# A convolution with a gate: 16 groups of six rows a step in place of 13, a second ScalarE copy for some halves, and one hand-ordered list

## The chip, the cores and the metric

The kernel runs on one core of a Trainium2 chip. A core has five engines with instruction queues of their own: TensorE (PE in the profile, its weight loads PEld), VectorE (DVE), ScalarE (ACT), GpSimd (POOL) and SyncE (SP, which here only issues transfers). Each engine works through its queue in order and waits on semaphores for the others. The metric is the device time of one execution in microseconds, the median of the runs shown.

## The reference

The reference is a causal convolution over time with three taps two steps apart, a gate, and an output projection:

```python
B, T, D, K = (2, 16000, 256, 3)       # x: B x T x D, w: K x D x 2D, w_o: D x D, all bf16
xp = jnp.pad(x, ((0, 0), (4, 0), (0, 0)))
h = sum over i of xp[:, off_i:off_i + T, :] @ w[i]     # off = 4, 2, 0 for i = 0, 1, 2
f, g = h[..., :D], h[..., D:]
z = jnp.tanh(f) * sigmoid(g)
return z @ w_o
```

So every row of the output needs three products of 256 x 512 and one of 256 x 256.

## The kernel before

**Groups.** Time is cut into groups. A group of kind B takes 4R consecutive rows, R at most 256, as 4 interleaved series of R columns; a group of kind A takes 6R rows as 6 series. One group, P, computes the first 640 rows of the first sequence directly with the three taps. A and B use shared products: sums and differences of the input rows are formed first, each is multiplied with a weight matrix (a tap, or a sum of taps) once, and the results are combined. A block is a quarter of a group: 128 of the 512 output channels of h. A block of B takes four products ("first" F, "last" L, "zero" Z, "inf" I) for two pairs of series; a block of A takes five (F, "mid" M, L, Z, I) for three pairs. Each product is two matrix multiplications of up to 512 columns (`product`, L386).

**The steps of a block.** F is added up in a PSUM bank b. ScalarE copies it to SBUF (ss, `copy_first`, L432; letter c in the plan). In an A block M is then added to the same bank and VectorE forms the half hh = 1.5 ss - b (`halfway`, L443; h). L is added to b. VectorE forms the start of another bank, a = 3 ss + b in an A block and -2 ss + b in a B block (L454; a), and in an A block also yy = 2 hh + b in SBUF (L457; y). Z is added to b, and I to a. ScalarE then applies tanh or sigmoid to b, yy and a (`activate`, L475), which gives th and sg. VectorE multiplies them (`gate`, L494; g). TensorE multiplies the result with w_o (`out_mm`, L512; P in the plan's TensorE part). ScalarE, at the very end also VectorE, copies that to SBUF (`out_evict`, L537 and L521; e and v), and SP's queue stores it (L540).

**The input sums.** `operand` (L325) lists them. For B: m, p, d0 and d3, each of two input rows. For A: u0, u1, u2, e and f of two input rows; u3, uh and ud are u1 times a constant; then rp = f + u1, rm = e + u3 and r0 = u0 + uh are made by transfers that POOL issues and that accumulate into f, e and u0 (`BY_DMA`), and ri = u2 + ud by POOL in four quarters. VectorE makes the A sums and part of the B sums, POOL makes the others in quarters. The input arrives by transposing transfers on SP's queue (`load`, L234) into four buffers for A and four for B.

**Buffers.** m, p, u3, uh and ud have two buffers each; d0, d3, u0, u1, u2, e and f have three. In PSUM bank b has three, a two, and the output product three.

**What sets the order.** `PLAN` (L13) is a text with one line per block slot and four parts in a line: TensorE, ScalarE, VectorE, GpSimd. Each engine gets its instructions in the order of its part, line by line. The blocks themselves are mixed by rule: four B groups first, then blocks of A and of B in turn, then the last B group. A POOL sum is issued just ahead of the a sum of its line and is held behind the last VectorE instruction, or the one or two before it (a ' for each); the code gives the reason as "GpSimd reads SBUF while VectorE's sums read PSUM". Loads are issued 15 slots ahead of their need, stores as soon as their last copy is issued. There are 13 A groups, 10 B groups of 256 columns, one of 160 and one of 128.

Of the kernel before, what the change touches and what calls it, by code (L numbers as in the profile page):

```python
# [11 lines left out]

PLAN = """  # L13
 |  | m.0 d3.0 p.0 d0.0 G | 
F D D | c w |  | 
F L D | c d | a d3.1 G | wa.4 wa.3
F L Z I P P | c b e | a | wa.6
Z L F I | a b c | m.1 d0.1 p.1 a | wa.12'
F L Z I | a c b | m.2 g a | wa.5
L P F Z I | a e c b | d3.2 a | wa.2'  # L20
Z L F I | a b c | d0.2 u0.0 g a | wa.7
F L Z I | a c b | f.0 u1.0 a | wa.1
L F Z I | a c b | p.2 a u2.0 g | wa.14'
L Z F I P | a b e c | e.0 d3.3 a | wa.0
F P P Z L I | a c e e b | p.3 ud.0 g a | wa.11
L F I Z P P | a c b | u1.1 m.3 m.4 a | rp.0 ri.0'
F L Z P I P | a e e e b c | u3.0 e.1 uh.0 a d0.3 f.2 g | wa.10
F I Z L P | a c e b | u1.2 a | rm.0 ri.0'
L F Z I | a e c b | a g | r0.0
L Z I F P | a b c | u3.1 p.4 a | wa.8  # L30
Z L F P I | a b c e e | u0.1 uh.2 f.1 a d0.4 g | ri.0'
F I L P Z M P | c e a b | d3.4 u2.1 ud.1 a h | rp.1 rm.1 wa.15' wa.13' wa.9'
F Z L M I | a c e e b | g uh.1 a y h | d3.5' d3.5' ri.0'
P P Z F L I | y a b c | u3.2 e.2 a y | r0.1 ri.1 m.5
F L I Z M | a c y b | a u0.2 h | d0.5 d0.5
Z F L I M | a b c e | g a y h | r0.2 d0.5 ri.1
F P Z I L | a e c b y | g u2.2 a y | rm.2 ri.1 m.5' d0.5
F L P I Z M | a e c y b | a e.3 h | p.5
Z F I L M | a c b | g a y h | p.5 p.5 ri.1
P P F Z L I | a e e y c b | u0.3 a y | m.5 m.5'  # L40
L F I Z M | a c y b | ud.2 a u1.3 h | ri.2 ri.2'
Z P P F L I P M | a b e c e e | g u3.3 a y h | rp.2 p.5' p.6' d0.6'
F Z I L P | a e b c y | f.3 g a y | ri.2 d3.5
F L I Z M | a c y b | a u2.3 h | d3.5
Z F I L M P P | a c b e | g a y h | rp.3 rm.3 d0.6 ri.2
F Z I L P | a e e y b c | uh.3 e.4 ud.3 a y | d3.6 p.6 ri.3''
F L I Z M | a c y b | a u1.4 h | ri.3
Z F I L M P P P | a c b e | g a y h | m.6 d3.6
F Z P L I | a e y c b e e e | g u0.4 u3.4 f.4 a y | r0.3 ri.3 m.6''
F L P I Z M | a c y b | a ud.4 h | d0.6 d3.6 m.6  # L50
Z I F L | a b c | g a y | ri.3 m.6
F L P I Z M P | c a y b | u2.4 a h | ri.4' d3.6
F Z L I P M | a e e c b | e.5 uh.4 y a h | rp.4 p.6
F Z P L I | a y c b e e | g f.5 a y | rm.4 p.6' d0.6'
F P L Z M I | a c y b | g a h | r0.4 p.7 p.7 ri.4 d3.7 d3.7 m.7
F Z L P M I | a c e b e | u1.5 a y h | ri.4
I Z P L F P P | a e e b c y | u0.5 a y | ri.4
F L Z I M | a c b y | ud.5 u1.6 u2.5 a h u3.5 g | rp.5 ri.5''
F P Z L I P M | a c e e b | a y h | rm.5 d0.7 p.7
F Z I L P | a e y b c e | g uh.5 a y | m.7' ri.5  # L60
F L I Z P M | a c y b | g ud.6 a h | r0.5 ri.5' m.7'
F P Z L M I | a c b e e | e.6 uh.6 y a h | d3.7 d0.7
F P Z L I P | y e a b c | f.6 a y | m.7' ri.5
F L Z M I P | a c y b e | u0.6 g h u3.6 a | rp.6 p.7' d0.7' d0.7
F L P M Z I | a c e e e b | y a h | rm.6
Z I L F P | a y b c | u2.6 u1.7 a y g | m.8' m.8'
F P P L Z M I | a c e y b e e | g u3.7 a h | r0.6 ri.6' d3.7'
F Z L P I M | a c b | e.7 ud.7 a y h | p.8' ri.6' ri.6
F Z I L P P | a y b c | u0.7 u2.7 a y | p.8' ri.6'
F L P M Z I | a e c y e e b | uh.7 f.7 a h g | d0.8' ri.7'  # L70
Z I F L | a b c | u1.8 a y | rm.7 rp.7 m.8'
F P P L Z M I | a c e y b e | g a e.8 h | d3.8 ri.7
F Z I L M P | a c b e | g a y ud.8 h | p.8 d3.8 ri.7
F P Z I L P | a e c y b e | u3.8 f.8 a y | r0.7 d3.8' d0.8
L F I Z M P | a e c b y | a u0.8 h | d0.8 m.8
F Z P L P M I P | a c e e e b | e.9 g a y h | p.8 ri.7
Z F L I | a b c y | u1.9 g a y | rp.8 d3.8
F L I Z M P P | a c e b y | u2.8 ud.9 a h | rm.8 d0.8 d3.9'
Z F L P M P I P | a e c e e b | uh.8 g a y h | ri.8 ri.8
Z L F I | y a b e c | u3.9 u2.9 a y | r0.8 ri.8  # L80
F I Z L M P P | a c y b | f.9 u0.9 a h | ri.9' ri.8'
F L Z I M | a e e c b | g y a h | ri.9
F Z I L | y a b c e | f.10 g a y | rp.9 d0.9
F P P L Z M I | c a b y | u0.10 a h | rm.9 d0.9'
F Z I L P P M | a e c e b | e.10 g uh.9 y a h | r0.9 d3.9
F P Z L P I | a e e y b c e | m.9 u1.10 a y | ri.9' ri.9
F L I Z M P | c a e b y | p.9 a h | d0.9' d3.9' d3.9'
Z P F L I M | a b c e e | ud.10 g a y h | d0.9
F I Z P L P | a y b c | u2.10 g a y | rp.10 ri.10 d3.10 d0.10
F L I Z M | a c e y b | a u1.11 h |   # L90
Z P F L P I | a b c e | u3.10 g y uh.10 a | rm.10 ri.10'
F L P Z I M | a e c b e y | e.11 a u2.11 h | ri.10'
F I Z L P P M | c a e b | ud.11 f.11 a y u3.11 h | r0.10 ri.10'
F I Z L | a e c y b e | g uh.11 a y | d3.10 d0.10'
L P F P Z M I | a c b y | g a h | rm.11 d0.10 d3.10
F Z L I M P | a c e b | u1.12 a y h | ri.11' ri.11'
F Z I L | a e c b y | p.10 m.10 y a | rp.11 ri.11
L P F P Z M I | a c e b y e | a u3.12 u0.11 h f.12 g | d3.10
Z F P L I P M P | a c b e | a y h | r0.11 ri.11 d0.10
I F Z L P | a e y e b e c | g e.12 ud.12 y a | rm.12  # L100
F P P M Z L P I | c e a b y e | p.11 u2.12 uh.12 a h g | d3.11' ri.12'
F I L P Z M P | a c e b | y a h | d0.11 d3.11
F Z L P I | y e a b c e e | u0.12 m.11 a y | rp.12 r0.12 ri.12''
F P Z L M I | c a b y | a h g | 
F Z L P I M P | a c b e e e | a y h | d0.11 ri.12
F Z L P I | a c b e y | g a y | d3.11 ri.12
L F I Z M P | a c y b e e | a g h | 
Z F L P I P M | b c a | y a h | 
F P Z L I | a e e y b c e | y a | d0.11
F P L Z M I | c a b y | a h g | d0.11  # L110
F P L Z I P | a e c b e | a y | d3.11
F I Z L | a c y b | g a | 
L P I F Z P | a e b c e | a g | 
Z I F L P P | a c b E | a v | 
L Z I P p | a b | a g v | 
Z I P p P | a e b | v | 
H H | a e E | g v | 
R R |  |  | 
 | e | v | 
# [4 lines left out]
def kernel(  # L124
# [7 lines left out]

    nc = tc.nc
# [15 lines left out]
    LOAD = 15  # L151
# [4 lines left out]
    LEAD, TRAIL = 4, 0  # L156
    N_A = (6, 7)
    groups, of_kind = [], {"P": [], "A": [], "B": []}

    def group(kind, b, t, R):  # L160
        of_kind[kind].append(len(groups))
        groups.append(dict(kind=kind, b=b, t0=t, R=R, J=ROWS[kind]))
        return t + ROWS[kind] * R

    for b in range(B):
        t = 0
        if b == 0:
            t = group("P", b, 0, 160)
        rows = (T - t - 6 * RG * N_A[b]) // 4
        n_a, n_b = N_A[b], rows // RG - (0 < rows % RG < P)  # L170
        for n in range(max(n_a, n_b)):
            if n < n_b:
                t = group("B", b, t, RG)
            if n < n_a:
                t = group("A", b, t, RG)
        rows = (T - t) // 4
        while rows:
            t = group("B", b, t, 160 if rows % P else P)
            rows = (T - t) // 4
    As, Bs = of_kind["A"], of_kind["B"]  # L180
    mixed = [[(g, oi) for g in gs for oi in range(4)] for gs in (As, Bs[LEAD:-1 - TRAIL])]
    seq = [(g, oi) for g in Bs[:LEAD] for oi in range(4)]
    took = [0, 0]
    while took != [len(m) for m in mixed]:
        nxt = 0 if took[0] * len(mixed[1]) < took[1] * len(mixed[0]) else 1
        seq.append(mixed[nxt][took[nxt]])
        took[nxt] += 1
    seq += [(g, oi) for g in Bs[-1 - TRAIL:] for oi in range(4)]
    slot_of = {blk: n for n, blk in enumerate(seq)}
    N = len(seq)  # L190
    assert N == 4 * (len(groups) - 1) == len(slot_of)
    begin = {g: slot_of[g, 0] for g in As + Bs}
    end = {g: slot_of[g, 3] for g in As + Bs}
# [5 lines left out]
    pre_pool = ctx.enter_context(tc.tile_pool(name="pre", bufs=2))  # L199
    dif_pool = ctx.enter_context(tc.tile_pool(name="dif", bufs=3))  # L200
    sum_pool = ctx.enter_context(tc.tile_pool(name="sum", bufs=2))
    ss_pool = ctx.enter_context(tc.tile_pool(name="ss", bufs=3))
# [314 lines left out]
    def out_evict(g, rb0, jp, on_v=False):  # L517
# [21 lines left out]
        if G["out", rb0] == J // 2:  # L539
            nc.sync.dma_start(  # L540
                out=out[G["b"], t0:t0 + J * P, :].rearrange("(p j) d -> p j d", j=J), in_=osb[:]
            )

# [179 lines left out]
```

## Time and profile before

| | |
|---|---|
| time, median of 3 runs | 263.12 us (263.03 to 263.28) |
| span of the profiled execution | 261.4 us; no other time of that execution is given |
| TensorE busy | 256.5 us, 98% |
| VectorE busy | 240.5 us, 92% |
| ScalarE busy | 243.7 us, 93% |
| GpSimd busy | 136.2 us, 52% |
| granted TensorE clock | 0.999 |
| transfers | 45.20 MB, 173 GB/s on average |

Busy time is the time in which at least one instruction of the engine runs; two instructions that overlap count once. The span goes from the first to the last instruction. In the rows of a group of instructions the mean is that of one instruction, overlap included. A row of the timeline gives start, length, engine, line and operation; "x2" behind it means that two like instructions are shown in one row, and a bracket gives the idle time ahead of it and what ended it.

### The profile page before, as it was taken

How to read it: one execution, taken by the hardware profiler on the slowest of the kernel's cores; microseconds unless marked ns; L12 is line 12 of the kernel's file. 1: busy time of each engine (PE TensorE's matmuls, PEld its weight loads, DVE VectorE, ACT ScalarE, POOL GpSimd, SP SyncE). 2: the span in 40 equal slices, each digit the busy share in tenths (PEclk: the TensorE clock that was granted, in tenths of full speed). 3: DMA queues.
4: the chain of work that ended last, by engine and by line, in shares of the span. 5: the costliest groups of instructions: out<-in, count | busy, mean ns of one | idle time of the engine just before them, and what ended most of it. 6: DMA issues, size and time to landing. Idle time of an engine off the chain costs nothing.

```text
span 261.4 us, 4534 instructions
## 1 busy us (share of the span) xinstructions
PE 256.5 (98%) x1484; PEld 144.2 (55%) x1484; DVE 240.5 (92%) x401; ACT 243.7 (93%) x492; POOL 136.2 (52%) x204
## 2 busy tenths in 40 slices
PE   8999999999999999999999999999999999999993
PEld 5654565545545555555555555555555555665682
DVE  2899999999999999999999999999999999977773
ACT  4989998999999999999999999999999999999993
POOL 1033355687765577956757685643746453431100
PEclk9999999999999999999999999999999999999999
DMA  6999979999969667969895799959825574462115
GB/s 185 215 168 212 262 177 174 227 211 179 212 152 232 139 147 143 228 147 230 197 197 135 175 214 190 239 160 201 237 41 127 149 152 116 129 160 109 76 61 210
DMA packets 81663, 45.20 MB, mean 173 GB/s; under 512 B 68936, under 2 KB 70216, under 8 KB 81640
## 3 DMA queue, kind: packets, MB, share of 16 engines
q1 hardware_dynamic: 75112, 33.74, 54.6%
q0 software_dynamic: 5616, 10.23, 23.2%
q10 hardware_dynamic: 912, 0.95, 1.1%
q8 instruction: 11, 0.18, 0.3%
q14 instruction: 12, 0.10, 0.1%
HBM read 1.25 MB, written 16.38 MB: 67 GB/s over the span
## 4 chain that ended last, share of the span: by engine, by line
PE 97%; DMA 1%; DVE 0%; issue 0%
PE b L401 57%; PE o_ps L512 21%; PE a L401 16%; PE b L421 1%; PE a L421 1%; DMA xn<-in_x_dram 1%; PE tp L308 0%; DVE osb L521 0%; PE fill L248 0%
## 5 line engine op out<-in xcount | busy, mean ns | idle before, releaser
L435 DVE SCALAR_TENSOR_TENSOR a<-ss,b 128x512 f32<-128x512 f32 (+2 forms) x100 | 67.1, 672 | 7.9 <-ACT sg L475 3.1
L537 ACT CAST osb<-o_ps 128x512 bf16<-128x512 f32 x119 | 69.8, 622 | 0.8 <-PE o_ps L512 0.7
L512 PE MATMUL o_ps<-wo_sb,zz 128*128 128x256 bf16 x496 | 70.5, 273 | 0.0
L432 ACT COPY ss<-b 128x512 f32<-128x512 f32 (+2 forms) x100 | 59.6, 597 | 4.6 <-PE b L401 3.5
L512 PEld LDWEIGHTS <-zz 128*128 128x128 bf16 x496 | 48.4, 98 | 25.2 <-DVE zz L494 0.2
L401 PEld LDWEIGHTS <-w_sb 128*128 128x128 bf16 x400 | 39.0, 98 | 36.8 <-issue 0.2
L382 POOL TENSOR_TENSOR u<-u,ud 128x256 bf16<-128x256 bf16 x52 | 39.8, 772 | 24.9 <-DVE zz L494 9.1
L382 POOL TENSOR_TENSOR d<-xt 128x256 bf16<-128x256 bf16 (+2 forms) x56 | 33.4, 606 | 32.7 <-DVE zz L494 13.0
L494 DVE TENSOR_TENSOR zz<-th,sg 128x1536 bf16<-128x1536 bf16 (+2 forms) x52 | 40.9, 788 | 0.5 <-ACT sg L475 0.2
L435 DVE SCALAR_TENSOR_TENSOR yy<-hh,b 128x512 f32<-128x512 f32 x52 | 35.4, 680 | 1.9 <-PE b L401 1.8
L435 DVE SCALAR_TENSOR_TENSOR hh<-ss,b 128x512 f32<-128x512 f32 x52 | 35.4, 681 | 1.2 <-PE o_ps L512 0.5
L475 ACT ACTIVATE sg<-b 128x512 bf16<-128x512 f32 (+2 forms) x50 | 30.5, 610 | 2.1 <-PE b L401 1.4
L475 ACT ACTIVATE th<-b 128x512 bf16<-128x512 f32 (+2 forms) x50 | 30.5, 610 | 1.9 <-PE b L401 1.6
L475 ACT ACTIVATE sg<-a 128x512 bf16<-128x512 f32 (+2 forms) x50 | 31.0, 619 | 0.0
L401 PE MATMUL b<-f,wp_sb 128*128 128x512 bf16 x104 | 30.9, 379 | 0.0
L401 PE MATMUL b<-u,w_sb 128*128 128x512 bf16 x104 | 30.9, 379 | 0.0
L401 PE MATMUL a<-u,w_sb 128*128 128x512 bf16 x104 | 30.9, 379 | 0.0
L401 PE MATMUL b<-u,wa_sb 128*128 128x512 bf16 x104 | 30.9, 379 | 0.0
L401 PE MATMUL b<-e,wm_sb 128*128 128x512 bf16 x104 | 30.9, 378 | 0.0
L475 ACT ACTIVATE th<-a 128x512 bf16<-128x512 f32 (+2 forms) x50 | 30.5, 614 | 0.3 <-PE a L401 0.2
L401 PEld LDWEIGHTS <-wp_sb 128*128 128x128 bf16 x200 | 19.5, 98 | 20.1 <-issue 0.7
L401 PEld LDWEIGHTS <-wm_sb 128*128 128x128 bf16 x200 | 19.5, 98 | 17.0 <-issue 0.4
(59 smaller groups left out, 342.7 us busy)
## 6 DMA issues: line engine op xcount, KB each, us to landing
out_dram<-osb SPq DMA_DIRECT2D x26, 384.0 KB, 2.6
out_dram<-osb SPq DMA_DIRECT2D x23, 256.0 KB, 3.0
f<-u POOLq DMA_DIRECT2D x13, 256.0 KB, 3.5
e<-u POOLq DMA_DIRECT2D x13, 256.0 KB, 4.4
u<-uh POOLq DMA_DIRECT2D x13, 256.0 KB, 5.3
w_sb<-in_w_dram ACTq DMA_DIRECT2D x3, 256.0 KB, 4.1
xt<-in_x_dram SPq DMA_TRANSPOSE x25, 7.2
xn<-in_x_dram SPq DMA_DIRECT2D x1, 160.0 KB, 3.2
```

Of the source, the lines that this page charges most:

```text
L382: ins = eng.tensor_tensor(out=o, in0=a, in1=b, op=op)
L401: nc.tensor.matmul(G[bank, oi][:, :2 * R], lhsT=wmat[:, ct, osl], rhs=G[mv][:, :, ct, :R], start=which == "first" and ct == 0, stop=ct == ...
L421: nc.tensor.matmul(G[bank, oi][:, :4 * r].rearrange("p (j r) -> p j r", j=4), lhsT=w_taps[tap][:, ct, osl], rhs=xt[:, j0:j0 + 4, ct, c0 + ...
L432: nc.scalar.copy(out=G["ss", oi][:, :n], in_=G["b", oi][:, :n])
L435: return note(nc.vector.scalar_tensor_tensor(out=out, in0=in0, scalar=scalar, in1=in1, op0=ALU.mult, op1=op))
L475: nc.scalar.activation(out=G[name, dt][:, j:j + 2, :R], in_=G[bank, oi][:, :2 * R].rearrange("p (q r) -> p q r", q=2), func=(ACT.Tanh, ACT ...
L494: note(nc.vector.tensor_tensor(out=G["z"][:, dt, :, :n], in0=G["th", dt][:, :, :n], in1=G["sg", dt][:, :, :n], op=ALU.mult))
L512: nc.tensor.matmul(o_ps[:, q, :], lhsT=z, rhs=wo_sb[:, dt, :], start=dt == 0 and (q == 0 or len(dts) == NT), stop=dt == NT - 1, skip_group ...
L537: copy(out=osb[:, 2 * jp:2 * jp + 2, :], in_=o_ps[:])
```

## The change

Five things change.

- The groups are written out. There are 16 A groups, 5 B groups of 256 columns, one of 160 and two of 128. P stays.
- The order of the blocks is written out too (`ORDER`): three B groups, then four A blocks to about one B block, then a B group of 128 columns.
- `PLAN` is one list of instructions of all engines in one order; each engine still takes its own in that order. Halves, evictions, stores (s) and loads (x) name what they handle, so that they need not come in the order of the blocks. A POOL sum carries a number q: it is held behind the VectorE instruction that many places back in the list (0 is the last).
- In 17 of the 64 A blocks the half is not formed on VectorE. ScalarE copies b a second time instead, after M (token k): hh = b. There yy = -2 hh + a, where a is the bank just formed as 3 ss + b; so yy comes after a, and it reads the bank a in PSUM before I is added to it. In the other 47 blocks h stays as it was.
- The buffers of the input sums, halves, activations and output rows are given out by the number of the group (`slot`), with the same counts as before; hh has three, as it had.

```diff
+GROUPS = (
+    "P160 A A A A A A A A B B B",
+    "A A A A A A A A B B B128 B160 B128",
+)
+ORDER = """
+9 9 9 9 10 10 10 10 11 11 11 11 1 20 1 1 1 2 20 2 2 2 3 20 3 3 3 4 20 4 4 4 5 21 5 5 5 6 21 6 6 6 7 21 7 7 7 8 21 8
...
 PLAN = """
- |  | m.0 d3.0 p.0 d0.0 G | 
-F D D | c w |  | 
...
+G p.0 m.0 d0.0 F d3.0 D c D d0.1 D F d p.1 L c G F w L A c P m.1 wa.2q1 x Z A I b wa.5q3 L u1.0 a wa.7q5 Z e0 F A
...
+b I Y e47 L a A F y P A Z c g Z b M b u1.7 F k25 I u0.7 c I u3.7 a L f.8 rm.7d M a A rp.7d P k26 ud.7 F e48 Y P
...
-    def halfway(blk):
+    def second(blk, on_act):
         g, oi = blk
         G = groups[g]
         n = 2 * G["R"]
-        G["hh", oi] = ss_pool.tile([P, 2 * RG], f32, name="hh")
+        G["hh", oi] = slot("hh", a_seq.index(blk), [P, 2 * RG], f32)
+        if on_act:
+            G["k", oi] = True
+            nc.scalar.copy(out=G["hh", oi][:, :n], in_=G["b", oi][:, :n])
+            return
         stt(G["hh", oi][:, :n], G["ss", oi][:, :n], 1.5, G["b", oi][:, :n], ALU.subtract)
...
             G["y", oi] = ss_pool.tile([P, 2 * RG], f32, name="yy")
-            stt(G["y", oi][:, :n], G["hh", oi][:, :n], 2.0, b)
+            if ("k", oi) in G:
+                stt(G["y", oi][:, :n], G["hh", oi][:, :n], -2.0, G["a", oi][:, :n])
+            else:
+                stt(G["y", oi][:, :n], G["hh", oi][:, :n], 2.0, b)
...
+    SLOTS = {"m": 2, "p": 2, "d0": 3, "d3": 3, "u0": 3, "u1": 3, "u2": 3, "e": 3, "f": 3, "u3": 2, "uh": 2, "ud": 2, "hh": 3, "th": 2, "osb": 3, "odd": 3}
+    def slot(name, n, shape, dtype=bf16, kind=None):
+        return ring_pool.tile(shape, dtype, name=name, tag=f"{name}.{n % SLOTS[kind or name]}")
...
+    def on_gpsimd(token):
+        token, _, back = token.partition("q")
+        behind = made_v[-1 - int(back)]
...
+    def store(g, rb0, odd):
...
+        nc.sync.dma_start(out=to, in_=G["osb", (rb0, odd)][:])
...
+    for token in PLAN.split():
+        what = token[0]
+        if "." in token:
+            if "q" in token:
+                on_gpsimd(token)
+            elif token[-1] == "d":
+                pre(*group_of(token[:-1]), None)
+            else:
+                note(pre(*group_of(token), nc.vector))
+        elif what in "FMLZI":
+            product(next(kinds[what]), {"F": "first", "M": "mid", "L": "last", "Z": "zero", "I": "inf"}[what])
...
+        elif what in "hk":
+            second(a_seq[int(token[1:])], what == "k")
```

More of the change, by code (lines that the diff above doesn't have):

```diff
@@ L150 @@
     BRIDGE, FILL = 4, 6
-    LOAD = 15
     W_A = 4
     ROWS = {"P": 4, "B": 4, "A": 6}
-    LEAD, TRAIL = 4, 0
-    N_A = (6, 7)
     groups, of_kind = [], {"P": [], "A": [], "B": []}
[L160 to L163, printed above, removed]
     for b in range(B):
         t = 0
[L167 to L189, printed above, removed]
-    N = len(seq)
-    assert N == 4 * (len(groups) - 1) == len(slot_of)
-    begin = {g: slot_of[g, 0] for g in As + Bs}
-    end = {g: slot_of[g, 3] for g in As + Bs}
+        for word in GROUPS[b].split():
+            kind, R = word[0], int(word[1:] or RG)
+            of_kind[kind].append(len(groups))
+            groups.append(dict(kind=kind, b=b, t0=t, R=R, J=ROWS[kind]))
+            t += ROWS[kind] * R
+        assert t == T
+    seq = []
+    for word in ORDER.split():
+        g = int(word)
+        seq.append((g, sum(at[0] == g for at in seq)))
+    As, Bs = ([g for g, oi in seq if oi == 0 and g in of_kind[kind]] for kind in "AB")
+    N = len(seq)
+    assert sorted(seq) == [(g, oi) for g in range(1, len(groups)) for oi in range(4)]
+    for gs in (As, Bs):
+        for n, g in enumerate(gs):
+            groups[g]["n"] = n
+    begin = {g: seq.index((g, 0)) for g in As + Bs}
     wanted = {g: begin[g] - (6 if g in As else 0) for g in As + Bs}
@@ L276 @@
     wm_sb = consts.tile([P, CT, D2], bf16)
[L277 removed]
+    wu_sb = [[slot("hh", tap, [P, D2], f32), ss_pool.tile([P, D2], f32, name="yy")] for tap in range(K)]
     wa_sb = consts.tile([P, CT, D2], bf16)
@@ L465, in activate @@
         if (name, dt) not in G:
-            G[name, dt] = act_pool.tile([P, J, RG], bf16, name=name, tag=f"{name}{J}")
+            same = [at for at in blocks if groups[at]["J"] == J]
+            G[name, dt] = slot(f"{name}{J}", NT * same.index(g) + dt, [P, J, RG], kind="th")
         if G["kind"] == "P":
@@ L705 @@
+    assert next(todo, None) is None and next(to_load, None) is None
 _INS = ['x', 'w', 'w_o']
```

346 lines of the change are left out of this document (116 added, 230 removed).

## The prediction

> **What bounds the kernel now.** I read the page first (engines, slices, chain), then the chain in order of time, then windows of the steady part, then single instructions.
>
> ```profile
> span 261.4 us, 4534 instructions
> PE 256.5 (98%) x1484; PEld 144.2 (55%) x1484; DVE 240.5 (92%) x401; ACT 243.7 (93%) x492; POOL 136.2 (52%) x204
> ...
> PE   8999999999999999999999999999999999999993
> ...
> DVE  2899999999999999999999999999999999977773
> ACT  4989998999999999999999999999999999999993
> ...
> PE 97%; DMA 1%; DVE 0%; issue 0%
> ...
> ```
>
> The chain is TensorE from end to end. A busy TensorE alone proves little, so I check its pace in the chain in order of time:
>
> ```profile
> 11.44 0.43 PE b L401 x2
> ...
> 47.98 1.73 PE b L401 x8
> ...
> 255.12 2.20 PE o_ps L512 x20
> ...
> 257.34 0.69 DVE osb L521
> ```
>
> A 512-column product takes 1.73/8 = 0.216 us, a 256-column one 2.20/20 = 0.110 us, in proportion to the columns, so it streams without gaps. Summing the plan of the kernel before, letter by letter, with these two prices (320 columns in proportion: 0.136) gives 244.8 us for TensorE. The plan's first product starts at 11.44 and the last ends at 257.32: 245.9 us. So TensorE waits 1.1 us in the whole plan. After it come 4.1 us of last copy and store (261.4 - 257.32).
>
> VectorE is next. The windows give DVE busy in the third pair of numbers behind the length (PE, PEld, DVE, ACT, POOL):
>
> ```profile
> 20.00:60.00 40.00, 40.00 (x217) 21.00 (x215) 39.55 (x68) 37.51 (x74) 22.08 (x32) 1.00 1.10 207
> ...
> 180.00:220.00 40.00, 40.00 (x228) 22.15 (x227) 38.75 (x66) 38.56 (x78) 20.81 (x30) 1.00 0.61 143
> 220.00:240.00 20.00, 20.00 (x125) 12.01 (x123) 17.51 (x31) 19.88 (x44) 7.18 (x12) 1.00 0.46 125
> 240.00:257.40 17.40, 17.30 (x132) 12.68 (x130) 12.79 (x24) 16.89 (x42) 1.20 (x3) 1.00 0.27 105
> ```
>
> Busy time overstates the load, because one instruction's end overlaps the next one's start. What an instruction costs its engine is the distance from start to start when the next is ready:
>
> ```profile
> 9.31 0.69 DVE L382 TENSOR_TENSOR m<-xt 128x1024 bf16<-128x1024 bf16 x1
> ...
> 100.59 0.68 DVE L494 TENSOR_TENSOR zz<-th,sg 128x1024 bf16<-128x1024 bf16 x1
> 101.19 0.69 DVE L382 TENSOR_TENSOR f<-xt 128x1024 bf16<-128x1024 bf16 x1
> 101.80 0.68 DVE L435 SCALAR_TENSOR_TENSOR a<-ss,b 128x512 f32<-128x512 f32 x1
> 102.40 0.68 DVE L435 SCALAR_TENSOR_TENSOR yy<-hh,b 128x512 f32<-128x512 f32 x1
> 103.00 0.95 DVE L494 TENSOR_TENSOR zz<-th,sg 128x1536 bf16<-128x1536 bf16 x1
> 103.87 0.69 DVE L435 SCALAR_TENSOR_TENSOR a<-ss,b 128x512 f32<-128x512 f32 x1
> ...
> 113.16 0.42 DVE L380 TENSOR_SCALAR u<-u 128x1024 bf16<-128x1024 bf16 x1
> 113.50 0.95 DVE L494 TENSOR_TENSOR zz<-th,sg 128x1536 bf16<-128x1536 bf16 x1
> ...
> 253.82 0.43 DVE L435 SCALAR_TENSOR_TENSOR a<-ss,b 128x256 f32<-128x256 f32 x1
> 254.16 0.42 DVE L494 TENSOR_TENSOR zz<-th,sg 128x512 bf16<-128x512 bf16 x1
> 254.49 1.28 DVE L521 CAST osb<-o_ps 128x512 bf16<-128x512 f32 x2
> ```
>
> So on VectorE: PSUM sum of 512 columns 0.60, of 256 columns 0.34; input sum of 1024 0.61; scaling 0.34; gate of 1536 0.87, of 1024 0.60, of 512 0.33; eviction 0.60. With these the VectorE plan sums to 228.8 us, between 9.31 and 257.94: 19.8 us are free, 7.1 of them after 220 us (2.49 + 4.61 in the last two windows), 12.7 spread before.
>
> **The change, part by part.** *TensorE.* Counted in the two programs: the products of 512 columns fall from 840 to 800 (13 x 40 + 10 x 32 against 16 x 40 + 5 x 32), those of 256 columns in B groups rise from 32 to 64; 320-column products, the direct group and the 500 output products stay. -40 x 0.216 + 32 x 0.110 = **-5.1 us**, all on the path. The new list sums to 239.7 us. With today's start, waits and tail: 11.44 + 239.7 + 1.1 + 4.1 = 256.3 us of span. That is the floor.
>
> *VectorE.* PSUM sums of 512 columns: a 92 to 84, halves 52 to 47, yy 52 to 64: -1 x 0.60 = -0.6. Of 256 columns 4 to 8: +1.4. Input sums of 1024: u 39 to 48, e and f 13 to 16 each, d 10 to 8, m and p 6 to 4 each: +9 x 0.61 = +5.5. Scalings 39 to 48: +3.1. Gates: 1536 26 to 32, +5.2; 1024 20 to 10, -6.0; 512 6 to 8, +0.7. Evictions 5 to 7: +1.2. Four short B sums become one: -1.1 (estimate, 0.37 each). Sum **+9.4 us**; summed token by token the list is 238.1 (+9.3). Today this would be hidden under TensorE's 12.7 us of cover, but TensorE gets 5.1 shorter too: the cover is gone. The two lists now run side by side: at the 32nd of 96 Z products TensorE's sum is 78.5 and VectorE's 79.8, at the 64th 160.8 and 161.2, at the 88th 222.6 and 223.1. VectorE starts 2.1 us earlier (9.31 against 11.44), and that is all its lead.
>
> *ScalarE.*
>
> ```profile
> 100.40 0.58 ACT L432 COPY ss<-b 128x512 f32<-128x512 f32 x1
> 100.88 0.60 ACT L475 ACTIVATE sg<-b 128x512 bf16<-128x512 f32 x1
> ...
> 103.27 0.69 ACT L475 ACTIVATE th<-yy 128x512 bf16<-128x512 f32 x1
> 103.81 0.64 ACT L475 ACTIVATE th<-b 128x512 bf16<-128x512 f32 x1
> ...
> 253.63 0.43 ACT L475 ACTIVATE th<-b 128x256 bf16<-128x256 f32 x1
> 253.91 0.43 ACT L475 ACTIVATE th<-a 128x256 bf16<-128x256 f32 x1
> ```
>
> 0.48 for 512 columns, 0.54 from yy, 0.28 for 256. Copies ss 92 to 84, new second copies +17, activations of a and b 184 to 168, of yy 52 to 64, evictions 119 to 117: +3 x 0.48, +12 x 0.06 for the yy, +12 x 0.28 for the 256-column ones: **+5.5 us**. The list sums to about 235, starting near 11.6: done at 247 of 256, so some 9 us of cover remain and I cost it at nothing. Without that cover it would add up to its 5.5.
>
> *The second copy (17 of 64 blocks).* It takes 0.60 off VectorE and puts 0.48 on ScalarE, and adds one wait: yy now reads the a bank, so the I product, which adds to that bank, waits for Y and not for A alone. Behind I the whole TensorE queue stands, since the order is fixed. By the sums between Y's end and I's start lie 1.0 to 3.7 us in these blocks, so no cost while VectorE is less than 1 us late; beyond that the excess, at most one sum (0.60) a block, 17 x 0.6 = 10 at the very worst, 0 at best. I take 0: it is part of how late VectorE is, below.
>
> *GpSimd, queues.* POOL's sums fall from 140 to 124, many of them shorter, its accumulating transfers rise from 39 to 48.
>
> ```profile
> 105.06 0.98 DVE L382 TENSOR_TENSOR u<-xt 128x1024 bf16<-128x1024 bf16 x1
> ...
> 105.45 1.11 POOL L382 TENSOR_TENSOR u<-u,ud 128x256 bf16<-128x256 bf16 x1
> ...
> L382 POOL TENSOR_TENSOR u<-u,ud x52: 658/667/1125, 33.1 to 236.4; 128x256 bf16<-128x256 bf16 x52
> L382 DVE TENSOR_TENSOR u<-xt x39: 673/685/1215, 21.7 to 227.8; 128x1024 bf16<-128x1024 bf16 x39
> ...
> f<-u POOLq DMA_DIRECT2D x13, 256.0 KB, 3.5
> e<-u POOLq DMA_DIRECT2D x13, 256.0 KB, 4.4
> u<-uh POOLq DMA_DIRECT2D x13, 256.0 KB, 5.3
> ...
> xt<-in_x_dram SPq DMA_TRANSPOSE x25, 7.2
> ```
>
> POOL at 52% has room. From issue to first use the new list leaves 5.2 to 17 us by TensorE's sum (the old plan 3.5 to 23), against 3.5 to 5.3 to land. Loads go from 25 to 24 transposes, SP's stores from 51 to 48, each load put by hand between stores; most stand 8 us or more ahead of the first use against 7.2 to land, one (the first 128-row B group that is mixed in) only 4 us, and there POOL waits with the transfers behind it. Cost 0 with 5 us on POOL; 2 to 6 if a late accumulation stops TensorE.
>
> The old plan put every POOL sum directly ahead of an a sum and held it behind one of the last three VectorE instructions. In the new list most holds name an instruction long past, so the start is where POOL's queue happens to be. 111 of 140 POOL sums and weight sums still stand ahead of a PSUM sum, 29 ahead of another kind. The rows above show what meeting costs: u took 0.98 where 0.69 is usual, and POOL's sum 1.11. If all 29 met: 29 x 0.29 = 8.4; if none, 0. I take 9 of them, 2.6, because in the rows of u the median stays at 685.
>
> *The sum.* Let x be the time VectorE does not run at its back-to-back pace up to the 88th block. Then span = 9.31 + 223.1 + x + 17.1 (TensorE's rest) + 4.1 = 253.6 + x, or the floor of 256.3 where x is under 2.7. Lower bound: 0.45 idle in 40 us (20 to 60, the one stretch where both plans already weigh the same), 2.4 over 214 us. Upper bound: the 12.7 us that VectorE stands idle today. The lower is nearer, as much of the 12.7 is waiting for a TensorE that was the bound: 2.4 + 2.6 for POOL = 5.0. Span 258.6. No separate time of the profiled execution is given; its span is 1.7 below the median of the runs (263.12 - 261.4), and I carry that: **260.3 us**, 1.1% faster.
>
> **The rivals.** *TensorE stays the bound* (x under 2.7): 256.3 + 1.7 = 258.0. For it, the 20-to-60 stretch, where TensorE did not wait; against it, that this lasted 40 us and would have to last 215.
>
> *VectorE becomes the bound (slower).* Place: the mixed stretch from 35 to 235 us; price: x stays at what it is today, 12.7: 266.3 + 1.7 = 268.0. It decides from x = 7.8 on, where 253.6 + x passes 261.4. For it: two lists of equal length that wait for each other in fixed order, with 2.1 us of lead; against it: TensorE was the bound while VectorE stood idle, so much of the 12.7 will not come again. The Trainium skill (Perfetto Trace Analysis, section "Identifying the Most-Contended Engine") judges VectorE and ScalarE by occupancy and does not count matmul occupancy: by it the 93% and 92% are the bound and a change that adds to both loses; the trace bears this out only in part, since TensorE streams at 0.216 a product.
>
> *VectorE and POOL exclude each other (slower).* Each of the 29 meetings makes VectorE wait out a whole POOL sum (667 ns in the row above): 2.4 + 19.3 = 21.7, 253.6 + 21.7 + 1.7 = 277.0. Against it: u has 685 as median although POOL is busy half of the time, and the u at 105.06 lost 0.29. The Trainium skill (SBUF — State Buffer, section "SBUF: two separate sides") states this rule, an exclusive lock on a shared pair of ports for operations with two SBUF inputs; the trace agrees that meetings cost, at less than half of that size.
>
> *The saving is given back*: x between 7.3 and 8.3, 262.6 to 263.6.
>
> *A late transfer*: two stops of about 3 us each at fixed products, 258.6 + 6 + 1.7 = 266.3. For it, 23% more accumulations; against it, the leads above.
>
> **How the numbers follow.** TensorE the bound 0.13; my forecast, x from 2.7 to 7.3 (258.0 to 262.6), 0.50; given back 0.10; VectorE the bound 0.16; POOL excluding VectorE 0.03; late transfer 0.08. A measurement here can tell about 0.2%, 0.5 us. Faster 0.63, same 0.10, slower 0.27. The range, 257.8 to 266.2, leaves out half of VectorE's case, the whole of POOL's and half of the late transfers, 0.15; the forecast's own range is 258.0 to 262.6.
>
> **What would show it.** TensorE's busy time near 251.4 if its sum is right. VectorE at 39.5 or more of 40 us in every window from 20 to 220. New waits of TensorE's loads on VectorE's a and yy, or none. If u, e and f last over 0.75 on average, the POOL part was too small; if the waits name DMA into f, e or u, it was the transfers; if ScalarE has no idle time and others wait for ss, the 9 us of cover were wrong.

## The result, and the profile after

The changed kernel takes 290.86 us (median of 4 executions, 289.38 to 293.16) against 263.2 us for the kernel before (263.03 to 263.28): **1.105 times as long, 95% interval 1.100 to 1.110**. The forecast was 260.3 us, faster. So 27.7 us were added where 2.8 were to be saved, and the sum missed 30.6 us. Single executions far off the others of their kernel (688 to 946 us in four, 270.7 and 274.6 us in two) are left out of every time, and the profiles of e2_own, e3_pace_own and e16_no_acc_ri, which are of such executions, are not read.

The page of the kernel after (engines, three of the slices, the granted clock, the chain):

```profile
span 291.4 us, 4595 instructions
...
PE 261.5 (90%) x1476; PEld 144.6 (50%) x1476; DVE 265.7 (91%) x419; ACT 249.1 (85%) x507; POOL 126.1 (43%) x197
...
PE   8799964999794999999989989987799989998994
...
DVE  3689971899999799999999999999999999998794
...
PEclk9979996999998899999999999999999999999999
...
PE 31%; DVE 24%; issue 10%; ACT 9%; DVEq 0%; ACTq 0%
```

TensorE was the chain for 97% before and is it for 31% now, with VectorE next. VectorE is busy 25.2 us longer than before, though its list should have grown by 9.3. The windows (length; busy time and instructions of PE, PEld, DVE, ACT, POOL; granted clock, share and GB/s of the transfers) show two different troubles:

```profile
40.00:60.00 20.00, 14.03 (x67) 7.11 (x65) 11.57 (x20) 11.04 (x22) 7.14 (x11) 0.83 0.53 104
...
140.00:180.00 40.00, 37.11 (x209) 20.26 (x208) 40.00 (x64) 36.97 (x76) 19.43 (x30) 1.00 0.98 201
180.00:220.00 40.00, 35.84 (x209) 20.13 (x208) 39.97 (x62) 36.39 (x77) 20.04 (x33) 1.00 0.88 195
```

From 40 to 60 us every engine is idle for a good part of the time. From 140 on VectorE is full and TensorE is not. The count alone does not say why: the kernel before got 64 and 66 VectorE instructions done in the last two of these windows, against 64 and 62, but VectorE had 1.2 us to spare in each and TensorE none:

```profile
140.00:180.00 40.00, 40.00 (x228) 22.05 (x227) 38.85 (x64) 38.43 (x77) 26.00 (x35) 1.00 0.85 181
```

The groups of VectorE's instructions tell more (count, busy us, mean ns of one, idle time ahead); first the kernel before:

```profile
L435 DVE SCALAR_TENSOR_TENSOR a<-ss,b 128x512 f32<-128x512 f32 x92 | 63.4, 690 | 3.9 <-PE b L401 2.6 <-ACT th L475 0.6
...
L382 DVE TENSOR_TENSOR u<-xt 128x1024 bf16<-128x1024 bf16 x39 | 27.9, 720 | 0.0
L494 DVE TENSOR_TENSOR zz<-th,sg 128x1536 bf16<-128x1536 bf16 x26 | 24.8, 954 | 0.5 <-ACT sg L475 0.2
L494 DVE TENSOR_TENSOR zz<-th,sg 128x1024 bf16<-128x1024 bf16 x20 | 13.7, 683 | 0.0
...
L380 DVE TENSOR_SCALAR uh<-u 128x1024 bf16<-128x1024 bf16 x13 | 5.5, 420 | 0.0
```

And the kernel after:

```profile
L368 DVE SCALAR_TENSOR_TENSOR a<-ss,b 128x512 f32<-128x512 f32 x84 | 57.4, 686 | 11.0 <-PE b L334 10.0 <-ACT th L416 0.6 <-PE a L334 0.3
L315 DVE TENSOR_TENSOR u<-xt 128x1024 bf16<-128x1024 bf16 x48 | 39.3, 829 | 0.0
L435 DVE TENSOR_TENSOR zz<-th,sg 128x1536 bf16<-128x1536 bf16 x32 | 36.4, 1137 | 0.0
...
L313 DVE TENSOR_SCALAR uh<-u 128x1024 bf16<-128x1024 bf16 x16 | 10.8, 673 | 0.0
L435 DVE TENSOR_TENSOR zz<-th,sg 128x1024 bf16<-128x1024 bf16 x10 | 8.9, 893 | 0.0
```

Sums with one operand in PSUM kept their time (a: 690 ns before, 686 now). Much of what works from SBUF alone became longer on average: u by 109 ns, the gate zz of 1536 by 183, that of 1024 by 210, uh by 253. These means come from few instructions: over the whole timeline 23 of VectorE's lasted more than 0.1 us beyond the usual length of their row, 22.2 us together, and all 23 overlap a GpSimd sum; the rest kept their length. In the kernel before there were 7, worth 1.8 us. The rise of uh is a single instruction, and the timeline of VectorE and of GpSimd (start, length, engine) shows what it waited for:

```profile
86.76 0.68 DVE L368 SCALAR_TENSOR_TENSOR hh<-ss,b 128x512 f32<-128x512 f32 x1
87.36 4.55 DVE L313 TENSOR_SCALAR uh<-u 128x1024 bf16<-128x1024 bf16 x1
91.83 0.68 DVE L368 SCALAR_TENSOR_TENSOR hh<-ss,b 128x512 f32<-128x512 f32 x1
...
86.43 0.96 POOL L315 TENSOR_TENSOR p<-xt 128x256 bf16<-128x256 bf16 x1
87.06 1.57 POOL L315 TENSOR_TENSOR u<-u,ud 128x256 bf16<-128x256 bf16 x2
88.31 0.94 POOL L315 TENSOR_TENSOR p<-xt 128x256 bf16<-128x256 bf16 x1
88.94 0.93 POOL L315 TENSOR_TENSOR u<-u,ud 128x256 bf16<-128x256 bf16 x1
89.56 0.93 POOL L315 TENSOR_TENSOR p<-xt 128x256 bf16<-128x256 bf16 x1
90.19 1.43 POOL L315 TENSOR_TENSOR d<-xt 128x256 bf16<-128x256 bf16 x2
```

The half hh, one operand in PSUM, runs beside GpSimd in its usual 0.68 us. The scaling uh, from SBUF to SBUF, takes 4.55 us instead of 0.42 and ends 0.3 us after GpSimd's run of sums does. GpSimd had saved up these sums while it waited, and nothing held them any more behind a late VectorE instruction.

The stop at 40 us is another thing. The waits (engine, line, waited for what; us, times, longest) and the instruction that waited:

```profile
PE b L334 <- DVE hh L368: 10.7, 6, 3.8
...
ACT hh L378 <- POOL wa_sb L231: 6.4, 1, 6.4
PE b L334 <- ACT hh L378: 6.0, 1, 6.0
```

```profile
45.74 1.07 POOL L231 TENSOR_TENSOR wa_sb<-hh 128x128 bf16<-128x128 f32 x1
...
46.84 0.59 ACT L378 COPY hh<-b 128x512 f32<-128x512 f32 x1 [6.37 <-POOL wa_sb L231]
```

The first second copy k0 writes a buffer of the ring hh. The scratch of the weights (wu_sb) lies in the same three buffers, so k0 must wait until GpSimd has formed the last piece of wa, at the end of its queue of those 40 us. TensorE stands behind k0 for 6.0 us, and its granted clock is 0.50 from 45.5 to 52.2 us: a product that took 0.59 us before the stop takes 1.06 there. The kernel before kept the scratch in the same three buffers; there the first half came at 47.85 us, beside the last sums of wa (46.94 to 48.33), and TensorE ran on.

### The profile page after: what moved, and what is told of

Read it like the earlier page. It is cut to its first block, busy times and chain, and to the rows that moved or that the text cites. A ratio compares the mean times of both kernels' runs of the same rounds, so it can differ in the third digit from the quotient of the medians.

```text
span 291.4 us, 4595 instructions
## 1 busy us (share of the span) xinstructions
PE 261.5 (90%) x1476; PEld 144.6 (50%) x1476; DVE 265.7 (91%) x419; ACT 249.1 (85%) x507; POOL 126.1 (43%) x197
## 4 chain that ended last, share of the span: by engine, by line
PE 31%; DVE 24%; issue 10%; ACT 9%; DVEq 0%; ACTq 0%
PE b L334 18%; PE o_ps L453 8%; DVE a L368 6%; PE a L334 5%; DVE yy L368 5%; DVE hh L368 4%; DVE zz L435 3%; DVE u L315 3%; ACT osb L470 2%; ACT th L416 2%; ACT sg L416 2%; ACT ss L365 2%; DVE e L315 1%; DVE u L313 1%; DVE uh L313 1%
## 5 line engine op out<-in xcount | busy, mean ns | idle before, releaser
L368 DVE SCALAR_TENSOR_TENSOR a<-ss,b 128x512 f32<-128x512 f32 (+2 forms) x96 | 62.6, 655 | 11.0 <-PE b L334 10.0
L315 POOL TENSOR_TENSOR u<-u,ud 128x256 bf16<-128x256 bf16 x64 | 49.1, 810 | 34.0 <-DVE u L315 24.5
L334 PE MATMUL b<-f,wp_sb 128*128 128x512 bf16 x128 | 38.5, 382 | 16.7 <-DVE hh L368 10.7
L435 DVE TENSOR_TENSOR zz<-th,sg 128x1536 bf16<-128x1536 bf16 (+2 forms) x50 | 48.7, 973 | 0.6 <-ACT sg L416 0.6
L334 PE MATMUL b<-u,w_sb 128*128 128x512 bf16 x128 | 38.6, 385 | 3.5 <-DVE a L368 2.8
L334 PE MATMUL a<-u,w_sb 128*128 128x512 bf16 x128 | 38.6, 383 | 2.4 <-DVE a L368 2.2
L315 DVE TENSOR_TENSOR u<-xt 128x1024 bf16<-128x1024 bf16 x48 | 39.3, 829 | 0.0
L334 PE MATMUL b<-e,wm_sb 128*128 128x512 bf16 x128 | 38.3, 381 | 0.0
L334 PE MATMUL b<-u,wa_sb 128*128 128x512 bf16 x128 | 38.2, 384 | 0.0
L310 POOL DMA_DIRECT2D e<-u x16 | 15.6, 977 | 42.3 <-PE b L334 27.0
```

The lines of the kernel that those rows point to most:

```text
L310: return nc.gpsimd.dma_start(out=G[name][:, :, :, :R], in_=b, accum_op=op)
L315: ins = eng.tensor_tensor(out=o, in0=a, in1=b, op=op)
L334: nc.tensor.matmul(G[bank, oi][:, :2 * R], lhsT=wmat[:, ct, osl], rhs=G[mv][:, :, ct, :R], start=which == "first" and ct == 0, stop=ct == ...
L368: return note(nc.vector.scalar_tensor_tensor(out=out, in0=in0, scalar=scalar, in1=in1, op0=ALU.mult, op1=op))
L435: note(nc.vector.tensor_tensor(out=G["z"][:, dt, :, :n], in0=G["th", dt][:, :, :n], in1=G["sg", dt][:, :, :n], op=ALU.mult))
```

## The experiments

All are compared with the kernel before, on the same chip (263.1 to 263.4 us in each batch). The times of most repaired kernels spread by 1 to 4 us, so a difference of 1 us between two of them tells nothing.

**The weights' scratch out of the halves' buffers (e2_own).** It shares the buffers of the six-row output rows instead.

```diff
-    wu_sb = [[slot("hh", tap, [P, D2], f32), ...
+    wu_sb = [[slot("osb6", tap, [P, D2], f32, kind="osb"), ...
```

> The changed kernel, with the scratch of the A weights taken out of the buffers of the halves (it shares the buffers of the 6-row output rows instead). Theory P (ports): two faults add up, the first second copy waits 6 us for GpSimd's weight sums (and TensorE behind it), and GpSimd's sums that start where the queue happens to be hold VectorE up for some 20 us. Here only the first goes: 283 to 286 us, and the stop of 6 us near 41 us is gone; u stays above 0.80 us and the gate of 1536 above 1.08. Theory L (lists): the two lists of equal length simply cannot both run dense; the early stop is only moved, and the time stays above 288.

Measured: 284.1 us (281.5 to 284.9), 1.076 [1.070, 1.082]. So the wait of k0 costs 6.8 us, the 6.0 of the row and a little more. Its own lengths and waits are not shown; in e4, built on it, TensorE is busy for 18.69 of the 20 us from 40 to 60, against 14.03.

**GpSimd paced again (e3_pace_own).** With e2's edit, every GpSimd sum is also held behind the VectorE instruction just ahead of it in the list; the numbers q are ignored.

```diff
-        behind = made_v[-1 - int(back)]
+        behind = made_v[-1]
```

> As the run before, and every GpSimd sum is held behind the last VectorE instruction ahead of it in the list (q = 0 for all), which is the pacing of the kernel before. Theory P: u comes down to 0.75 or less and the gate of 1536 to 1.00 or less, and the time to 264 to 271 us. Theory L: the means fall too, but the time stays above 278, since VectorE only waits elsewhere.

Measured: 270.1 us (269.9 to 271.4), 1.027 [1.024, 1.030]. One line gives back 14.0 us. The lengths are read in e4 below, which has the same hold: u falls from 829 to 734 ns, the gate of 1536 from 1137 to 1014.

**The opposite in the kernel before (e7_before_free).** All its GpSimd sums are held behind VectorE's first instruction, which means not at all.

```diff
-            behind = made_v[-1 - token.count("'")]
+            behind = made_v[0]
```

> The kernel before, with the hold of every GpSimd sum set to VectorE's first instruction, so that GpSimd starts as soon as its operands are there; nothing else is changed. Theory P: the gate of 1536 goes from 0.954 us to above 1.02 and u from 0.72 to above 0.78, VectorE loses 8 to 15 us, of which 12 are covered today: 264 to 272 us. Theory L: the means stay within 0.03 us and the time within 1 us of 263.

Measured: 315.4 us, 1.197 [1.196, 1.199]. VectorE's groups in this kernel:

```profile
L435 DVE SCALAR_TENSOR_TENSOR a<-ss,b 128x512 f32<-128x512 f32 x92 | 63.0, 687 | 9.4 <-PE b L401 8.7 <-ACT th L475 0.4
L494 DVE TENSOR_TENSOR zz<-th,sg 128x1536 bf16<-128x1536 bf16 x26 | 39.1, 1504 | 0.8 <-ACT sg L475 0.7
...
L494 DVE TENSOR_TENSOR zz<-th,sg 128x1024 bf16<-128x1024 bf16 x20 | 25.9, 1297 | 0.0
```

The direction was expected, the size by far not: the holds are worth 52 us to a kernel that changes in nothing else. The a sums stay at 687 ns; the gates go from 954 to 1504 and from 683 to 1297. 47 instructions are longer than usual by over 0.1 us, 48.8 us together against 1.8 before, and all of them overlap a GpSimd sum. This is the clearest evidence for the cause, since neither groups nor lists differ from the kernel before.

**GpSimd's sums placed just ahead of PSUM sums (e4_align_own).** On top of e3, a GpSimd sum waits in the list until the next a, yy or half, at the latest until the product that needs it.

```diff
+        elif "." not in token and what in "AYh" and waiting:
+            on_gpsimd(waiting.pop(0))
...
-                on_gpsimd(token)
+                waiting.append(token)
```

> As the run before, and each GpSimd sum also waits in the list until the next a, yy or half sum of VectorE comes, one GpSimd sum ahead of each. Theory P: below the run before by 1 to 4 us, 260 to 269, u at 0.72 or less. Theory L: like the run before, above 278.

Measured: 271.2 us (269.4 to 272.8), 1.026 [1.022, 1.030]: no gain over e3 that could be told. Being held behind any late VectorE instruction is what counts. Meetings are left, but shorter ones: 28 instructions, 8.0 us together.

**Two tries to let GpSimd meet PSUM sums alone (e8_two_own, e13_halves).** In e8 (built on e3) a sum is only put where two PSUM sums follow each other; e13 (built on e12_both, below) cuts it in two where just one does.

```diff
+            if waiting and (two or len(waiting) > 4 and "." not in token and what in "AYh"):
+                on_gpsimd(waiting.pop(0))
```

```diff
+                if part is None and big and not two and len(waiting) < 5:
+                    on_gpsimd(token_, 0)
+                    waiting[0] = (token_, 1)
```

> As the aligned kernel, but a GpSimd sum is issued only where two PSUM sums of VectorE follow each other (or where more than four are waiting), since a GpSimd sum (0.67 us) is longer than one PSUM sum (0.60). If the rest of VectorE's loss is the overhang: u at 0.71 or less, gate of 1536 at 0.98 or less, 264 to 269 us. If GpSimd then comes late for TensorE: 270 to 276.

> As the run before, and a GpSimd sum of 256 columns is cut into two of 128 (0.40 us in place of 0.67) wherever the PSUM sum that covers it is not followed by another. Theory P: what is left of VectorE's longer instructions is the overhang of the GpSimd sum into the next VectorE instruction: the gate of 1536 goes to 0.97 or less, u to 0.70 or less, 3 to 5 us off, 259 to 263 us. If GpSimd comes late instead: 266 or more.

Measured: 297.1 us, 1.128 [1.126, 1.131], and 285.7 us, 1.086 [1.082, 1.089]. Both made it worse. The waits of e8:

```profile
PE a L334 <- POOL u L315: 18.4, 16, 3.1
```

and of e13:

```profile
PE a L339 <- POOL u L320: 16.2, 16, 3.1
```

TensorE's I product now waits for ri, once in each of the 16 groups. There are not enough such places: a more careful pacing makes GpSimd late.

**VectorE's share of it (e6_no_k, e9_more_k).** Both are e4 with another number of second copies on ScalarE: none instead of 17, which puts 17 halves of 0.60 us back on VectorE, and 30 instead of 17. The edit of e6:

```diff
-            second(a_seq[int(token[1:])], what == "k")
+            second(a_seq[int(token[1:])], False)
```

> The paced and aligned kernel with all 64 halves on VectorE (no second copies). If VectorE's back-to-back work is now the bound, its 17 x 0.60 = 10 us come in full or nearly: 276 to 282 us. If waits are the bound and not VectorE's work: 268 to 273.

> The aligned kernel with 13 more second copies on ScalarE (30 of 64). If VectorE is the bound: 13 x 0.60 = 8 us less for it and 6 more for ScalarE, 263 to 267 us. If ScalarE or the waits are the bound: 269 to 275.

Measured: 279.65 us, 1.063 [1.061, 1.065] without them, 8.4 above e4 for 10.2 us of work; 272.8 us, 1.037 [1.035, 1.039] with 30, 1.6 above. So the 17 copies are worth about their price, and more of them bring nothing: in two windows of e9_more_k

```profile
60.00:100.00 40.00, 38.76 (x216) 20.92 (x215) 37.21 (x61) 38.59 (x79) 25.20 (x36) 1.00 0.74 165
100.00:140.00 40.00, 39.72 (x218) 20.95 (x216) 38.63 (x64) 39.83 (x82) 20.18 (x30) 1.00 0.84 175
```

VectorE has room (37.21 and 38.63 of 40), and ScalarE is the fuller of the two (38.59 and 39.83).

**Loads earlier, first gate later (e10_loads, e12_both).** In e4 a load for a B group came late. e10 moves the last four loads for B groups up by two or three places; e12 also puts the first gate, which VectorE reaches first and must wait for, behind three input sums.

```diff
+    for late, ahead in ((21, 5), (23, 12), (22, 15), (24, 17)):
+        loads.remove(late)
+        loads.insert(loads.index(ahead), late)
...
-G p.0 m.0 d0.0 F d3.0 D ...
+m.0 p.0 d0.0 G F d3.0 D ...
```

> The aligned kernel (269 to 272 us) with the loads of the four mixed B groups put one to three places earlier among the loads; nothing else. Theory D: the stop near 175 us, where GpSimd waits for a late load and TensorE for the transfer of r0 behind it, is a cost of its own: 265 to 268 us. Theory V: VectorE's work alone sets the time, and the stop is made up elsewhere: 269 or more.

> As the run before, and the first gate of group P comes behind the sums m, p and d0 of the first B group, as in the kernel before, where it stood first in the list and waited for ScalarE. Theory S: the 2.2 us that TensorE loses in the first 20 us come back: 2 us below the run before, 263 to 266. Theory V: no difference beyond 0.5 us.

Measured: 272.8 us, 1.036 [1.034, 1.039], and 271.3 us, 1.033 [1.028, 1.037]. Nothing was gained. A stop of TensorE between 180 and 190 us went (busy 8.48 of 10 us in e4, 9.88 in e12), and another came between 200 and 210 (9.77 in e4, 6.68 in e12). The window of e12_both there, then its timeline and the transfers issued from 185 to 206 us (KB each, median us from issue to landing):

```profile
200.00:220.00 20.00, 16.68 (x98) 9.38 (x97) 17.23 (x29) 16.81 (x37) 10.08 (x17) 1.00 0.68 146
```

```profile
187.36 10.80 SPq L169 DMA_TRANSPOSE xt<-in_x_dram  x2
...
193.51 0.88 POOL L313 DMA_DIRECT2D e<-u  x1 [0.86 <-DVE e L318]
...
203.65 0.60 PE L337 MATMUL b<-e,wm_sb 128*128 128x512 bf16 x2 [3.32 <-DMA e<-u]
```

```profile
e<-u POOLq DMA_DIRECT2D x1, 256.0 KB, 10.1
xt<-in_x_dram SPq DMA_TRANSPOSE x2, 9.6
...
e<-u POOLq DMA_DIRECT2D x16, 256.0 KB, 4.3
```

An accumulation into e was issued at 193.51, while two transposing loads were running, and landed after 10.1 us; the last row gives 4.3 us as the median over the whole execution. TensorE stood 3.3 us for it. Moving a load moved the meeting, and with it the stop.

**GpSimd's last sums away (e5_no_ri, e14_no_ri_fixed).** The 64 sums of ri are left out, in e4 and in e12, to measure the contact that is left between GpSimd and VectorE. These kernels and those below no longer compute the reference's output.

```diff
+        if name == "ri":
+            return None
```

> The paced and aligned kernel of the runs before, with GpSimd's 64 quarters of ri = u2 + ud left out (the I products of the A blocks then read u2 alone). It measures what is left of GpSimd's sums. If what remains above the floor is VectorE and TensorE waiting on GpSimd (VectorE's longer instructions, 8 us, and TensorE's waits on POOL and DMA, 5 us): 258 to 263 us, u at 0.71 or less. If the two equal lists alone cost it: 267 or more.

> The kernel of the two fixes (loads and first gate), with GpSimd's 64 quarters of ri left out (the I products of the A blocks read u2 alone). The lists with almost no GpSimd: if the two equal lists can run side by side, 259 to 262 us, the prediction's own sum (260.3); if not, 264 or more.

Measured: 269.3 us, 1.022 [1.018, 1.026], and 270.8 us, 1.025 [1.018, 1.032]: 1.9 and 0.6 us, where about 10 had been expected. The idea that the rest was still GpSimd beside VectorE alone fell with this. u is down to 687 ns, and TensorE's waits in e14_no_ri_fixed now name transfers:

```profile
PEld L339 <- DMA e<-u: 6.2, 3, 3.4
...
PE b L339 <- DMA e<-u: 4.9, 3, 2.9
```

**The accumulating transfers away, with controls (e15_no_acc, e16_no_acc_ri, e20_no_acc_ri_again, e17_before_no_acc_ri, e18_before_no_acc).** rp, rm and r0 are left as f, e and u0; e16, e17 and e20 leave out ri too. e17 and e18 are the kernel before, the others e12; e20 is the same kernel as e16.

```diff
         if eng is None:
+            return None
+        if False:
             return nc.gpsimd.dma_start(out=G[name][:, :, :, :R], in_=b, accum_op=op)
```

> The repaired new list with its first gate moved and four loads earlier (269 to 272 us) without the 48 accumulating transfers (rp, rm and r0 are left as f, e and u0, so the output is not the reference's); GpSimd's sums for ri stay. Theory T, late accumulations are what holds the repaired list up: the stop in the slice from 200 to 220 us goes (TensorE over 19 of 20 there, 16.7 with the transfers), 260 to 264 us. Theory V, VectorE and the lists' order hold it: 268 to 272, and the waits of TensorE name VectorE.

> The same without the 64 GpSimd sums for ri as well (u2 is left as it is, so the output is not the reference's): two lists without transfers and nearly without GpSimd. T: 257 to 261 us, the floor of the prediction's sum. V: 267 to 270, as without ri alone (270.8).

> The run without accumulations and without the sums for ri again (262.1 us), for a profile of it: if VectorE's list at its limit is the rest, VectorE is busy 39.5 or more of 40 us in the windows from 60 to 220 us with means of its sums as in the kernel before (u 690, gate of 1536 columns 955 ns), and TensorE is not; if TensorE is the bound, its chain is TensorE for over 90% as in the kernel before.

> The kernel before, without its 39 accumulating transfers and its GpSimd sums for ri (output not the reference's): the control for the run above. Both theories: TensorE waited for 1.1 us in the whole plan, so 262 to 263.5 us. If the new list without both lies below this one, the saving of 5.1 us on TensorE is real and the side streams hid it; if it lies above, it is VectorE's list.

> The kernel before without its 39 accumulating transfers, GpSimd's sums for ri kept (output not the reference's): 262 to 263.5 us by both theories; more than 1 us below 263.2 would say that transfers cost the kernel before too.

| without | new list, repaired (e12) | kernel before |
|---|---|---|
| nothing | 271.3 us | 263.1 us |
| accumulations | 265.6 us, 1.010 [1.008, 1.012] | 263.6 us, 1.002 [1.001, 1.003] |
| accumulations and ri | 262.1 and 262.5 us, 0.997 [0.996, 0.998] | 263.0 us, 1.000 [0.998, 1.001] |

The side streams cost the kernel before nothing, and the repaired new list 9.2 us. Taken alone, ri was worth 0.6; once the accumulations are away it is worth 3.5, so the two are not to be priced one by one. The window of e15_no_acc where e12 stopped:

```profile
200.00:220.00 20.00, 19.89 (x120) 11.42 (x118) 19.96 (x35) 19.94 (x44) 6.98 (x13) 1.00 0.17 63
```

What is left without both is a draw of two lists. The windows of e20_no_acc_ri_again:

```profile
60.00:100.00 40.00, 40.00 (x230) 22.32 (x229) 40.00 (x68) 39.74 (x81) 10.09 (x17) 1.00 0.57 145
100.00:140.00 40.00, 40.00 (x223) 21.48 (x221) 39.84 (x68) 39.65 (x81) 4.26 (x9) 1.00 0.47 122
140.00:180.00 40.00, 38.87 (x231) 22.33 (x230) 38.54 (x68) 39.02 (x83) 8.39 (x18) 1.00 0.51 124
180.00:220.00 40.00, 40.00 (x235) 22.69 (x233) 39.86 (x71) 40.00 (x87) 5.46 (x13) 1.00 0.42 123
```

TensorE, VectorE and ScalarE are all full or nearly so, with 68 to 71 VectorE instructions in 40 us. The chain is TensorE for 85%, below the 90% of the expectation, and VectorE for 6%; no engine alone is shown as the bound.

**Late landing or late issue (e19_no_late_loads).** In e12, 16 of the 24 loads are left out; the groups read rows of an earlier group again.

```diff
+        if G["kind"] != "P" and len(filled[J]) == 4:
+            G["xt"] = [xt for xt, rows in filled[J] if rows >= R][G["n"] % 2]
+            return
```

> The repaired new list with its first gate moved and four loads earlier (269 to 272 us), with 16 of its 24 transposing loads left out: those groups read the rows of an earlier group again, so the output is not the reference's. All sums and accumulations stay. Theory C, the accumulations land late because a transposing load fills the transfer engines beside them: the 48 accumulations all land in under 7 us (9 to 10 at the stops with the loads), the stop between 200 and 220 us goes, 265.5 to 268 us, near the run without accumulations (265.6). Theory R, they are late because VectorE or GpSimd issues them late: 269 to 272 us, and the stop stays.

Measured: 267.9 us (267.2 to 268.1), 1.018 [1.017, 1.020]: 3.4 of the 5.7 us. The window, and the accumulations' median landing over the execution:

```profile
200.00:220.00 20.00, 19.44 (x113) 10.76 (x112) 19.97 (x34) 19.54 (x42) 10.04 (x17) 1.00 0.46 113
```

```profile
e<-u POOLq DMA_DIRECT2D x16, 256.0 KB, 3.6
u<-uh POOLq DMA_DIRECT2D x16, 256.0 KB, 3.4
```

The stop is gone, with GpSimd's issues waiting for TensorE's products on bank b as long as in e12 (25.1 us in 9 waits in both). The accumulation into e that was issued at 193.51 us in e12 is issued at 193.55 here, after the same wait, and lands after 4.0 us in place of 10.1; its row for the time from 193.4 to 194 us:

```profile
e<-u POOLq DMA_DIRECT2D x1, 256.0 KB, 4.0
```

So this stop comes from an accumulation that lands beside transposing loads. The other 2.3 us of the accumulations have not been told apart.

No version that computes the reference's output beat the kernel before; the best were e3_pace_own, e4_align_own and e12_both at 270.1 to 271.3 us.

## Why the prediction was wrong

Going down the chain of runs, the 30.6 us between 260.3 and 290.9 are: 6.8 for k0 and the weights' scratch (e2), 14.0 for unpaced GpSimd (e3), -1.2 for placement, loads and gate (e4 and e12, which gained nothing), 5.7 for the accumulations (e15), 3.5 for ri behind them (e16), and 1.8 between the lists alone and the forecast (262.1 - 260.3). Each is the price at its place in this order.

- **The step that failed first is "GpSimd, queues".** It saw that most holds name an instruction long past, and then counted neighbours in the list (29 of 140), let 9 of them meet and priced a meeting at 0.29 us: 2.6 us, where pacing gave back 14.0. Without a hold the list says nothing of when GpSimd runs, so any VectorE sum, gate or scaling on SBUF can meet it: 11 of 48 u sums and 10 of 32 gates of 1536 did, and they lasted 1.32 us against 0.68 and 1.55 against 0.95 of those that met nothing. These are means of meetings that cost nothing and of meetings that cost up to 2.1 us, for VectorE waits out what GpSimd has lined up; the scaling uh lost 4.1 us. The 23 that became longer lost 0.96 us each, more than a whole GpSimd sum (median 667 ns in the kernel before). The step also took from the u median of 685 in the kernel before that few of them would meet. It was the pacing that kept the meetings rare there, which e7 shows: 52 us.
- **The rival "VectorE and POOL exclude each other"**, given 0.03, had the right mechanism. The Trainium skill (SBUF — State Buffer, section "SBUF: two separate sides") has the shared port pair as an exclusive lock, and names the VectorE operations that need it: those with two SBUF inputs and those in a two-port fast mode. The trace agrees, with the PSUM sums at 686 ns and the gates at 1137; whether uh, which has one input, runs in such a mode no run here shows. The rival's price, 19.3 us for 29 meetings of 667 ns, is near the 22.2 measured by luck: there were fewer long meetings, and each cost more. The argument against it, that u kept its median while GpSimd was busy half of the time, was drawn from a kernel built to avoid the meetings.
- **"The second copy", taken at 0.** The step looked at the wait of I for Y and did not ask whose buffers k writes. The new list puts the first half ahead of the last weight sums, whose scratch lies in the halves' buffers: 6.8 us, at one place. By the code a half on VectorE would write the same buffer, so it would be the place in the list that costs, and not the engine; no run tests that.
- **"Cost 0 with 5 us on POOL; 2 to 6 if a late accumulation stops TensorE."** The upper case came true in the repaired list: 5.7 us. In the changed kernel itself TensorE's longest wait for an accumulation is 0.5 us. The leads of 5 us and more that the step counted were fair against a median landing of 3.5 to 5.3 us, not against the 10.1 us of the one beside two transposing loads.
- **The list term, x = 2.4 without GpSimd, was too small as well.** The counts of instructions on the three engines are as the prediction has them. With the side streams away the sum would say the floor, 256.3 us of span; e20 has 260.5, so x in "span = 253.6 + x" is 6.9, of which 1.1 us are meetings that are left. The 1.8 us in the chain above look small only because the forecast holds 2.6 for GpSimd. The new list gains 0.5 to 0.9 us over the kernel before without its side streams (262.1 and 262.5 against 263.0), not the 5.1 of TensorE. Which waits make up the rest stays open.
- **VectorE the bound** came true from 140 us on, by waiting and not by work: VectorE's busy time is 265.7 us in the kernel after and 245.4 in e20 for the same 419 instructions. The Trainium skill (Perfetto Trace Analysis, section "Identifying the Most-Contended Engine") judges VectorE and ScalarE by their occupancy. At 92% and 93% in the kernel before they had little room for anything to be late, as the full windows of e20 show.

Of the signs that were named, u, e and f did last over 0.75 us on average (829, 793 and 743 ns, 805 over all 80), which meant that the GpSimd part was too small. TensorE's busy time, named as near 251.4 us, was 261.5, and 253.9 in e20.

## What to carry to other kernels

When a list is rewritten, ask of every wait what else it did beside keeping the order: here the holds of GpSimd were the pacing that kept it off VectorE's SBUF work, and a hold that points to the past is no hold. When an instruction moves to another engine, look up which buffers it writes and who else uses them. A side stream that costs nothing beside one bound engine can cost when several engines run level, as here 9.2 us: leave it out in both kernels and compare before pricing it.

## What the hardware showed beyond that

- VectorE does not only lose one GpSimd sum in a meeting. A 0.42 us scaling waited through seven back-to-back GpSimd sums, 4.55 us, without getting in between two of them.
- GpSimd's issuing of an accumulating transfer (about 0.9 us) is no such meeting: 34 sums, gates and scalings of the kernel after ran beside nothing else of GpSimd, and none lasted over 0.01 us longer.
- The granted TensorE clock fell to 0.83 in the window from 40 to 60 us (0.50 from 45.5 to 52.2), in which TensorE was idle for 6 us, and was 1.00 from 20 to 40 us and from 100 us on.
- An accumulating transfer of 256 KB took 10.1 us beside two transposing loads, and the same transfer 4.0 us with these loads away.
